# A transformer block on one core: weight loads issued in the written order, dummy matmuls at the start, and a reordered first layer norm

## The chip, the cores and the metric

The kernel runs on one core of one Trainium2 chip. The metric is the device time of one execution in microseconds (us). All engines of the core run their own instruction lists side by side and meet only at semaphores: TensorE (PE in the rows; its weight loads are listed apart as PEld), VectorE (DVE), ScalarE (ACT), GpSimd (POOL), and SyncE (SP), which here only issues DMA transfers. The 16 DMA engines of the core carry out what SP, ACT and POOL issue.

## The reference

One block of a diffusion transformer, for 2 images of 256 tokens of width D = 1152, with 2 heads of 576, in bf16:

```
mod = (silu(c) @ w_mod)            -> shift_a, scale_a, gate_a, shift_m, scale_m, gate_m
h   = layernorm(x) * (1 + scale_a) + shift_a
q, k, v = h @ wqkv                 ; attn = softmax(q k^T / sqrt(576))
x   = x + gate_a * ((attn @ v) @ wo)
h2  = layernorm(x) * (1 + scale_m) + shift_m
out = x + gate_m * (gelu(h2 @ w_fc1) @ w_fc2)
```

w_mod is 1152 x 6912, wqkv 1152 x 3456, wo 1152 x 1152, w_fc1 1152 x 4608, w_fc2 4608 x 1152. Every weight is read once; the whole read is 50 MB.

## The kernel before, in words

**Tiling.** The 512 tokens are four tiles t of 128. The width 1152 is nine pieces kt of 128 rows. A weight slice 1152 x 1152 takes one region of 20736 bytes a partition in the on-chip memory, and regions are used again: region A holds the scale slice of w_mod (`WSC`) and later the query weights (`WQ`); B holds the key weights (`WK`) and later `WO`; C the shift slice (`WSH`) and later the value weights (`WV`); a region of four times that size holds the other four slices of w_mod (`WMODR`) and later `WFC2`; `WFC1` comes back into A and C.

**Stages on TensorE**, in this order: the transposed c (`c_T`); the scale pieces `sc_0` to `sc_8` (each nine matmuls of 2 columns into one bank, one weight piece kt at a time), each followed by one or two dummy matmuls of 512 columns (`warm`), with the transposes of the normalised token tiles (`xnT_0` to `xnT_3`, nine of 128 x 128 each) between them; the first six column tiles of K, kt by kt; K tiles 6 and 7; the shift pieces `sh_0` to `sh_8`; K tile 8; nine tiles of Q (`proj(WQ, ...)`, lines 1006 to 1012) with scores and softmax between them; V; `rows` (line 901), which makes the other four modulation rows out of `WMODR`, kt by kt; attention times V; the output projection `wo`; the second layer norm; fc1 and fc2. K needs only the scale (`hk`, line 798: 18 VectorE pieces), Q and V also the shift (`hx`, lines 842 and 845: 6 pieces on ScalarE, 12 on VectorE).

**The first layer norm** (lines 701 to 737). Tiles 0 to 2 take their statistics on VectorE (three `bn_stats`, one aggregate), tile 3 on ScalarE (a square pass and a sum pass); 1/sqrt comes from GpSimd. Tile 0 is normalised on ScalarE (line 732, with -mean/sigma made in line 730), tiles 1 to 3 on VectorE (line 735).

**What sets the order.** The program is written as a list of units. `Sched.schedule` plays them in time with costs of its own and so fixes each engine's list. TensorE is held to the written order (`pe_seq`). On the other engines the planner takes, among the units whose inputs are ready at that moment of its model, the one with the highest priority. For SP the priority is the written order (`u.bl = 1e12 - u.uid`, line 305), but a load that is not ready yet is passed over. A load is not ready as long as the region that it writes is still read: `WQ` has to wait for the last matmul that reads `WSC`, `WV` for the last one that reads `WSH`, `WO` for K tile 8. `WMODR`'s region is free from the start. In the written order the loads are x, `WSC`, `WK`, `WSH`, `WQ` (two pieces, columns 0 to 383 and 384 to 1151, line 793), `WV` (line 832), `WMODR` (three pieces, line 834), `WO` (line 848), then `WFC1` pieces 0 and 1, 2 and 3, then `WFC2`.

On the chip SP issues its list strictly one after the other, and a DMA that waits for a semaphore holds all that stand behind it. The gate rows (`st_g`, `ld_g`) go out and come back through POOL's own queue.

Of the kernel before, what the change touches and what calls it, by code (L numbers as in the profile page):

```python
# [8 lines left out]
ENGINES = ("pe", "act", "dve", "pool", "sp")  # L9
# [162 lines left out]
class Sched:  # L172
# [107 lines left out]
    def schedule(self, dma_bw=385.0, dma_issue=650.0, dma_lat0=900.0, dma_lat1=600.0, verbose=False):  # L280
        units = self.units
        for u in units:
            for ins in u.instrs:
                for d in ins.deps:
                    if d.unit is not u:
                        u.deps.add(d.unit)
        for u in units:
            for d in u.deps:
                d.succ.add(u)
        pe_seq = [u for u in units if u.eng == "pe"]  # L290
        pe_next = {a.uid: b for a, b in zip(pe_seq, pe_seq[1:])}
        pe_pos = 0
        for u in reversed(units):
            m = 0.0
            for s in u.succ:
                if s.bl > m:
                    m = s.bl
            if u.uid in pe_next:
                m = max(m, pe_next[u.uid].bl)
            d = u.dur if u.dma_bytes == 0 else (u.dur + u.dma_bytes / dma_bw + dma_lat0 + dma_lat1)  # L300
            u.bl = d + m + u.prio_boost
        nsp = sum(1 for u in units if u.eng == "sp")
        for u in units:
            if u.eng == "sp":
                u.bl = 1e12 - u.uid
        ndeps = {u.uid: len(u.deps) for u in units}
        ready = {e: [] for e in ENGINES}
        avail_time = {}
        for u in units:
            if ndeps[u.uid] == 0:  # L310
                avail_time[u.uid] = 0.0
                ready[u.eng].append((-u.bl, u.uid))
        eng_free = {e: 0.0 for e in ENGINES}
        dma_free = 0.0
        events = []
        now = 0.0
        done = 0
        order = {e: [] for e in ENGINES}
        pending_fin = []
        n = len(units)  # L320
        scheduled = 0
        while scheduled < n:
            progressed = False
            for e in ENGINES:
                if eng_free[e] > now:
                    continue
                h = ready[e]
                if not h:
                    continue
                pick = None  # L330
                for it in h:
                    if e == "pe" and it[1] != pe_seq[pe_pos].uid:
                        continue
                    if avail_time[it[1]] <= now and (pick is None or it < pick):
                        pick = it
                if pick is None:
                    continue
                h.remove(pick)
                if e == "pe":
                    pe_pos += 1  # L340
                u = units[pick[1]]
                u.start = now
                if u.dma_bytes > 0:
                    u.end = now + u.dur
                    if e == "sp":
                        xs = max(u.end + dma_lat0, dma_free)
                        dma_free = xs + u.dma_bytes / dma_bw
                        u.fin = dma_free + dma_lat1
                    else:
                        u.fin = u.end + 1500.0 + u.dma_bytes / (dma_bw * 0.5) + dma_lat1  # L350
                else:
                    u.end = now + u.dur
                    u.fin = u.end + u.lat
                eng_free[e] = u.end
                order[e].append(u)
                pending_fin.append((u.fin, u.uid))
                scheduled += 1
                progressed = True
            fin_now = sorted(it for it in pending_fin if it[0] <= now)
            if fin_now:  # L360
                pending_fin = [it for it in pending_fin if it[0] > now]
            for f, uid in fin_now:
                for s in units[uid].succ:
                    ndeps[s.uid] -= 1
                    at = max(avail_time.get(s.uid, 0.0), f + (SEM_LAT if True else 0.0))
                    avail_time[s.uid] = at
                    if ndeps[s.uid] == 0:
                        ready[s.eng].append((-s.bl, s.uid))
                progressed = True
            if progressed:  # L370
                continue
            cands = []
            if pending_fin:
                cands.append(min(it[0] for it in pending_fin))
            for e in ENGINES:
                if eng_free[e] > now:
                    cands.append(eng_free[e])
                for it in ready[e]:
                    if avail_time[it[1]] > now:
                        cands.append(avail_time[it[1]])  # L380
            cands = [c for c in cands if c > now]
            if not cands:
                raise RuntimeError("scheduler stuck: %d/%d" % (scheduled, n))
            now = min(cands)
        self.order = order
        self.makespan = max(u.fin for u in units)
        return order

    def emit(self, nc, block, sems, dma_sems):
        order = self.order  # L390
# [101 lines left out]
D = 1152  # L492
KT = 9
# [27 lines left out]
def c_dve_fast(n):  # L521
    return 160.0 + 0.37 * n
# [10 lines left out]
def build_kernel(nc, x, c, wqkv, wo, w_mod, w_fc1, w_fc2, out):  # L533
# [5 lines left out]
    with (  # L539
# [14 lines left out]
        def ps16(bank, c0=0, n=1024):  # L554
            v = psum[:, bank * 512: (bank + 1) * 512].bitcast(BF16)
            return v[:, c0:c0 + n]
# [94 lines left out]
        def dve(cost, fn, reads, writes, name):  # L651
            return S.op("dve", cost, fn, reads=reads, writes=writes, name=name)
# [37 lines left out]

        S.op("pool", 100, lambda e: e.memset(NHALF, -0.5), writes=[NHALF], name="nhalf")

        CT_PS = ps16(7, 0, 18)
        S.unit("pe", 100, "c_T")
        tr(CT_PS, CSB[0:18, :], IDENT[0:18, 0:18])
# [25 lines left out]
        for t in range(4):  # L721
            xt, xn, mv, rs = X[:, t, :], XN[:, t, :], MV[:, t, :], RSTD[:, t:t + 1]
            if t < 3:
                ln_stats_dve(xt, [X[:, t, i * CH:(i + 1) * CH] for i in range(NCH)], BN[:, t, :], mv, rs, "ln1_%d" % t)
            else:
                ln_stats_act(xt, xn, mv, SUMS[:, 0:2], rs, "ln1_%d" % t)
            m = MV[:, t, 0:1]
            if t == 0:
                nm = NMR[:, t:t + 1]
                dve(170, lambda e, m=m, rs=rs, nm=nm: e.scalar_tensor_tensor(out=nm, in0=m, scalar=-1.0, in1=rs, op0=ALU.mult, op1=ALU.mult),  # L730
                    [m, rs], [nm], "nmr_%d" % t)
                act(1300, lambda e, xt=xt, xn=xn, rs=rs, nm=nm: e.activation(out=xn, in_=xt, func=ACTF.Identity, scale=rs, bias=nm),  # L732
                    [xt, rs, nm], [xn], "xn_%d" % t)
            else:
                dve(c_dve_fast(D), lambda e, xt=xt, xn=xn, m=m, rs=rs: e.tensor_scalar(out=xn, in0=xt, scalar1=m, scalar2=rs,
                                                                                     op0=ALU.subtract, op1=ALU.mult),
                    [xt, m, rs], [xn], "xn_%d" % t)


        XB = [(0, 1, 2), (3, 4, 6)]  # L740
# [10 lines left out]
                src = ps16(XB[b][q], 0, nk * 256).rearrange("p (k t) -> p k t", k=nk)  # L751
                copy_on(eng, HX[:, 4 * q:4 * q + nk, b * 256:(b + 1) * 256], src, nk * 256, True, "xnT_ev%d_%d" % (b, q))

        def warm(n, tag, src):
            for i in range(n):
                S.unit("pe", 300.0, "warm_%s_%d" % (tag, i))
                mm(ps32(5), IDENT, src, True, True)

        def mod_kt(W, kt, col0, name):
            S.unit("pe", 9 * 27.0, name)  # L760
# [1 line left out]
                mm(ps32(7, col0 + f * 2, 2), W[:, kt, f * 128:(f + 1) * 128], ST[:, kt:18:9], kt == 0 and f == 0, kt == KT - 1,  # L762
                   skip_group_check=True)

        mod_kt(WSC, 0, 0, "sc_0")
        warm(1, "a", WSC[:, 0, 0:512])
        xn_T(0)
        mod_kt(WSC, 1, 0, "sc_1")
        warm(1, "b", WSC[:, 1, 0:512])
        mod_kt(WSC, 2, 0, "sc_2")  # L770
        warm(1, "c", WSC[:, 2, 0:512])
        xn_T(1)
        mod_kt(WSC, 3, 0, "sc_3")
        warm(1, "d", WSC[:, 3, 0:512])
        mod_kt(WSC, 4, 0, "sc_4")
        warm(1, "e", WSC[:, 4, 0:512])
        xn_T(2)
        mod_kt(WSC, 5, 0, "sc_5")
        warm(1, "f", WSC[:, 5, 0:512])
        xn_T(3)  # L780
        mod_kt(WSC, 6, 0, "sc_6")
        warm(1, "g", WSC[:, 6, 0:512])
        mod_kt(WSC, 7, 0, "sc_7")
        warm(2, "h", WSC[:, 7, 0:512])
        mod_kt(WSC, 8, 0, "sc_8")
        warm(2, "i", WSC[:, 8, 0:512])
        xn_T_ev(0)
        xn_T_ev(1)
        MT0 = ps32(7, 0, 18)
# [33 lines left out]
            qk_evac(dst_j, bank)  # L823

        dve(330, lambda e: e.memset(QK[64:128, 4, :], 0.0), [], [QK[64:128, 4, :]], "z4a")
        dve(330, lambda e: e.memset(Q4B[0:64, :], 0.0), [], [Q4B[0:64, :]], "z4b")

        proj(WK, 6, 15, HK, 6)
        proj(WK, 7, 16, HK, 0)
# [305 lines left out]
```

## Time and profile before

| what | us |
|---|---|
| median of 3 runs | 276.48 |
| lowest, highest | 275.17, 277.48 |
| the profiled execution's own time | 275.82 |
| its span in the trace | 273.7 |
| TensorE busy in the span | 242.7 |
| VectorE, ScalarE, GpSimd busy | 68.5, 65.6, 19.6 |

All times in the rows are counted from the start of the span; 2.1 us of the execution lie around it. In a timeline a row is: start, duration, engine, line, operation, output <- inputs, count, and in brackets how long the engine was idle before and who released it. A row with a count above one stands for that many neighbouring instructions. In the list of transfers the last number is the time from the issue to the landing. The chain of waits is followed back from the last instruction; "issue" in it is time for which the trace shows no releaser.

### The profile page before, as it was taken

How to read it: one execution, taken by the hardware profiler on the slowest of the kernel's cores; microseconds unless marked ns; L12 is line 12 of the kernel's file. 1: busy time of each engine (PE TensorE's matmuls, PEld its weight loads, DVE VectorE, ACT ScalarE, POOL GpSimd, SP SyncE). 2: the span in 40 equal slices, each digit the busy share in tenths (PEclk: the TensorE clock that was granted, in tenths of full speed). 3: DMA queues.
4: the chain of work that ended last, by engine and by line, in shares of the span. 5: the costliest groups of instructions: out<-in, count | busy, mean ns of one | idle time of the engine just before them, and what ended most of it. 6: DMA issues, size and time to landing. Idle time of an engine off the chain costs nothing.

```text
span 273.7 us, 3973 instructions
## 1 busy us (share of the span) xinstructions
PE 242.7 (89%) x1734; PEld 143.8 (53%) x1746; DVE 68.5 (25%) x183; ACT 65.6 (24%) x128; POOL 19.6 (7%) x33
## 2 busy tenths in 40 slices
PE   0589980079989999999999999999999999999996
PEld 0464450034656557666976444444456666666675
DVE  5534231011534024689310000000001221111222
ACT  2540232002226225036953332323210000000000
POOL 1200000000000013575000000000000000000000
PEclk9999996569999999999999999999999999999999
DMA  6999999999664199993079644500000000000001
GB/s 223 387 392 399 428 415 424 379 378 392 244 203 146 25 398 394 389 364 120 0 264 362 188 121 152 166 0 0 2 0 14 17 14 29 17 14 14 17 16 29
DMA packets 27867, 51.57 MB, mean 188 GB/s; under 512 B 1479, under 2 KB 15559, under 8 KB 26699
## 3 DMA queue, kind: packets, MB, share of 16 engines
q1 hardware_dynamic: 27440, 50.14, 51.1%
q0 software_dynamic: 384, 1.19, 1.2%
q8 instruction: 13, 0.21, 0.3%
q14 instruction: 3, 0.02, 0.0%
q10 hardware_dynamic: 27, 0.00, 0.0%
HBM read 50.14 MB, written 1.19 MB: 188 GB/s over the span
## 4 chain that ended last, share of the span: by engine, by line
PE 88%; issue 6%; DVE 2%; DMA 2%; ACT 1%; SPq 0%
PE psum L667 85%; PE psum L670 3%; DMA arena<-in_x_dram 2%; DVE arena L845 1%; ACT arena L712 0%; ACT arena L732 0%; SPq L648 0%; DVE arena L990 0%; ACT arena L662 0%; DVE arena L971 0%; DVE arena L798 0%; DVE arena L1078 0%; DVE arena L1079 0%; ACT arena L713 0%; DVE arena L790 0%
## 5 line engine op out<-in xcount | busy, mean ns | idle before, releaser
L667 PE MATMUL psum<-arena 128*128 128x384 bf16 (+5 forms) x1627 | 237.0, 311 | 24.7 <-issue 16.1
L667 PEld LDWEIGHTS psum<-arena 128*128 128x128 bf16 (+1 forms) x1639 | 136.5, 98 | 120.9 <-issue 20.0
L1078 DVE TENSOR_TENSOR arena<-psum,arena 128x384 f32<-128x384 f32 (+1 forms) x14 | 7.0, 501 | 118.6 <-PE psum L667 118.6
L662 ACT ACTIVATE arena<-psum 128x512 bf16<-128x512 f32 (+6 forms) x34 | 19.0, 579 | 61.2 <-PE psum L667 61.2
L1003 ACT ACTIVATE arena<-psum 128x512 bf16<-128x512 f32 (+1 forms) x44 | 22.4, 523 | 43.3 <-PE psum L667 43.3
L664 DVE CAST arena<-psum 128x512 bf16<-128x512 f32 (+3 forms) x17 | 10.7, 643 | 48.9 <-PE psum L667 48.8
L670 PE MATMUL psum<-arena 128*128 128x128 bf16 (+2 forms) x107 | 9.6, 240 | 3.7 <-DMA arena<-in_c_dram 2.2
L972 POOL TENSOR_TENSOR arena<-arena 128x384 f32<-128x384 f32 x12 | 10.9, 910 | 10.1 <-DVE arena L971 9.0
L670 PEld LDWEIGHTS psum<-arena 128*128 128x128 bf16 (+2 forms) x107 | 8.0, 112 | 6.2 <-DMA arena<-in_c_dram 2.2
L704 DVE BATCH_NORM_STATS2 arena<-arena 128x6 f32<-128x384 f32 (+1 forms) x21 | 10.8, 543 | 0.4 <-DMA arena<-in_x_dram 0.4
L977 ACT ACTIVATE arena<-arena 128x1152 bf16<-128x1152 f32 x4 | 5.4, 1350 | 9.6 <-DVE arena L976 9.5
L971 DVE TENSOR_TENSOR arena<-psum,arena 128x384 f32<-128x384 f32 x12 | 6.6, 549 | 3.7 <-PE psum L667 3.6
L648 POOL DMA_DIRECT2D dit_scratch<-arena x2 | 1.3, 629 | 86.9 <-DVE arena L664 86.9
L1079 DVE TENSOR_TENSOR arena<-arena 128x384 bf16<-128x384 f32 (+1 forms) x14 | 7.0, 502 | 0.5
L993 ACT ACTIVATE arena<-psum,arena 128x128 bf16<-128x128 bf16 x16 | 6.1, 460 | 4.2 <-PE psum L670 4.0
L990 DVE TENSOR_SCALAR arena<-psum,arena 128x128 bf16<-128x128 bf16 x20 | 5.5, 335 | 4.5 <-PE psum L670 4.5
L870 ACT ACTIVATE arena<-psum,arena 128x256 bf16<-128x256 f32 x8 | 3.7, 470 | 7.7 <-DVE arena L867 4.9
L708 POOL TENSOR_TENSOR arena<-arena 128x1 f32<-128x1 f32 x7 | 3.9, 550 | 8.6 <-DVE arena L707 8.6
L866 DVE TENSOR_REDUCE arena<-psum 128x2 f32<-128x512 f32 x4 | 2.8, 692 | 6.0 <-PE psum L667 5.9
L842 ACT ACTIVATE arena<-arena 128x256 bf16<-128x256 bf16 x6 | 3.1, 586 | 4.3 <-DVE arena L836 4.3
L664 DVE COPY arena<-psum 128x256 bf16<-128x256 bf16 (+2 forms) x5 | 2.0, 423 | 6.6 <-PE psum L667 4.7
L798 DVE TENSOR_SCALAR arena<-arena 128x256 bf16<-128x256 bf16 x18 | 3.6, 281 | 0.0
(39 smaller groups left out, 28.0 us busy)
## 6 DMA issues: line engine op xcount, KB each, us to landing
arena<-in_w_mod_dram SPq DMA_DIRECT2D x3, 3456.0 KB, 26.5
arena<-in_w_fc_dram SPq DMA_DIRECT2D x9, 1152.0 KB, 8.1
arena<-in_w_fc_dram SPq DMA_DIRECT2D x4, 2592.0 KB, 14.9
arena<-in_w_mod_dram SPq DMA_DIRECT2D x9, 288.0 KB, 6.5
arena<-in_wqkv_dram SPq DMA_DIRECT2D x9, 288.0 KB, 7.9
arena<-in_w_mod_dram SPq DMA_DIRECT2D x3, 864.0 KB, 13.1
arena<-in_wqkv_dram SPq DMA_DIRECT2D x1, 2592.0 KB, 17.2
arena<-in_wo_dram SPq DMA_DIRECT2D x1, 2592.0 KB, 20.3
```

Of the source, the lines that this page charges most:

```text
L662: act(c_act(n), lambda e: e.activation(out=dst, in_=src, func=ACTF.Copy), [src], [dst], name)
L664: dve(c_dve_psum16(n) if psum16 else c_dve_psum32(n), lambda e: e.tensor_copy(dst, src), [src], [dst], name)
L667: S.instr(lambda e: e.matmul(o, lhsT=l, rhs=r, start=st, stop=sp, **kw), reads=[l, r], writes=[o])
L670: S.instr(lambda e: e.transpose(o, i_, idn), reads=[i_, idn], writes=[o])
L704: dve(550, lambda e, s=s, o=o: e.bn_stats(out=o, in_=s), [s], [o], "bn_%s_%d" % (tag, ci))
L971: dve(550, lambda e, o=o, ga=ga, x1c=x1c: e.tensor_tensor(out=x1c, in0=o, in1=ga, op=ALU.mult), [o, ga], [x1c], "wo_t1_%d_%d" % (t, ci))
L972: S.op("pool", 930, lambda e, xs=xs, x1c=x1c: e.tensor_tensor(out=x1c, in0=x1c, in1=xs, op=ALU.add), reads=[x1c, xs], writes=[x1c], name=" ...
L990: dve(335, lambda e, o=o, dst=dst, s1=s1, s2=s2: e.tensor_scalar(out=dst, in0=o, scalar1=s1, scalar2=s2, op0=ALU.mult, op1=ALU.add), [o, s ...
L993: act(440, lambda e, o=o, dst=dst, s1=s1, s2=s2: e.activation(out=dst, in_=o, func=ACTF.Identity, scale=s1, bias=s2), [o, s1, s2], [dst], ...
L1003: act(c_act(ntok), lambda e: e.activation(out=dst, in_=o, func=ACTF.Gelu_apprx_tanh), [o], [dst], "gelu_%d_%d" % (f, tok0))
L1078: dve(c_dve_psum32(w), lambda e, o=o, gm=gm, t1=t1: e.tensor_tensor(out=t1, in0=o, in1=gm, op=ALU.mult), [o, gm], [t1], "fc2_t1_%d_%d" % ( ...
L1079: dve(c_dve_32(w), lambda e, t1=t1, x1c=x1c, ost=ost: e.tensor_tensor(out=ost, in0=t1, in1=x1c, op=ALU.add), [t1, x1c], [ost], "fc2_out_%d ...
```

## The change

SP is now held to the written order as TensorE was: a load that is not ready holds the later ones in the planner's list. `Q4B` (512 columns, later half of a query tile) is zeroed first on VectorE; two dummy matmuls of 512 columns (identity times `Q4B`) stand before `c_T` and 22 after it, ahead of the first transposes. The dummy matmuls between the scale pieces read `Q4B` and no longer `WSC`: one after each piece and one at the end, and the transposes of tiles 1, 2, 3 follow `sc_1`, `sc_3`, `sc_5`. Tile 0 is normalised on VectorE like the others. A report function that runs only when asked for is added; it puts no instruction into the program.

```diff
-        pe_seq = [u for u in units if u.eng == "pe"]
-        pe_next = {a.uid: b for a, b in zip(pe_seq, pe_seq[1:])}
-        pe_pos = 0
+        seq = {e: [u for u in units if u.eng == e] for e in ("pe", "sp")}
+        pos = {"pe": 0, "sp": 0}
+        pe_next = {a.uid: b for a, b in zip(seq["pe"], seq["pe"][1:])}
...
-                    if e == "pe" and it[1] != pe_seq[pe_pos].uid:
+                    if e in seq and it[1] != seq[e][pos[e]].uid:
                         continue
...
-                if e == "pe":
-                    pe_pos += 1
+                if e in seq:
+                    pos[e] += 1
...
+        dve(600, lambda e: e.memset(Q4B, 0.0), [], [Q4B], "zq4b")
+        for i in range(2):
+            S.unit("pe", 430.0, "warm_a%d" % i)
+            mm(ps32(5), IDENT, Q4B, True, True)
...
-            if t == 0:
-                nm = NMR[:, t:t + 1]
-                dve(170, lambda e, m=m, rs=rs, nm=nm: e.scalar_tensor_tensor(out=nm, in0=m, scalar=-1.0, in1=rs, op0=ALU.mult, op1=ALU.mult),
-                    [m, rs], [nm], "nmr_%d" % t)
-                act(1300, lambda e, xt=xt, xn=xn, rs=rs, nm=nm: e.activation(out=xn, in_=xt, func=ACTF.Identity, scale=rs, bias=nm),
-                    [xt, rs, nm], [xn], "xn_%d" % t)
-            else:
-                dve(c_dve_fast(D), ...)
+            dve(c_dve_fast(D), lambda e, xt=xt, xn=xn, m=m, rs=rs: e.tensor_scalar(out=xn, in0=xt, scalar1=m, scalar2=rs,
+                                                                                 op0=ALU.subtract, op1=ALU.mult),
+                [xt, m, rs], [xn], "xn_%d" % t)
...
-        def warm(n, tag, src):
+        def warm(n, tag):
             for i in range(n):
-                S.unit("pe", 300.0, "warm_%s_%d" % (tag, i))
-                mm(ps32(5), IDENT, src, True, True)
+                S.unit("pe", 215.0, "warm_%s_%d" % (tag, i))
+                mm(ps32(5), IDENT, Q4B, True, True)
...
-        mod_kt(WSC, 0, 0, "sc_0")
-        warm(1, "a", WSC[:, 0, 0:512])
+        warm(22, "b")
         xn_T(0)
-        mod_kt(WSC, 1, 0, "sc_1")
-        warm(1, "b", WSC[:, 1, 0:512])
...
-        mod_kt(WSC, 8, 0, "sc_8")
-        warm(2, "i", WSC[:, 8, 0:512])
+        for kt in range(KT):
+            mod_kt(WSC, kt, 0, "sc_%d" % kt)
+            warm(1, "k%d" % kt)
+            if kt in (1, 3, 5):
+                xn_T((kt + 1) // 2)
+        warm(1, "e")
...
-        dve(330, lambda e: e.memset(Q4B[0:64, :], 0.0), [], [Q4B[0:64, :]], "z4b")
```

## Rows read from the trace of the kernel before

**Rows 1.** The page: shares of the chain that ended last, by engine.

```profile
PE 88%; issue 6%; DVE 2%; DMA 2%; ACT 1%; SPq 0%
```

**Rows 2.** The chain of waits in order: start, duration, what, count.

```profile
14.62 0.88 PE psum L667 x10
15.50 0.96 PE psum L670 x9
...
19.05 0.70 PE psum L667 x10
...
42.43 13.77 issue
...
121.86 0.50 PE psum L670 x9
...
146.40 10.74 PE psum L667 x49
```

**Rows 3.** Timeline of TensorE's matmuls, 0 to 60 us.

```profile
20.52 19.81 PE L667 MATMUL psum<-arena 128*128 128x512 bf16 x160 [0.43 <-DVE arena L798]
56.20 3.98 PE L667 MATMUL psum<-arena 128*128 128x512 bf16 x10 [15.87 <-issue]
```

**Rows 4.** Timeline of SP's issues: last of WSC and WSH, WMODR, then WQ.

```profile
7.68 0.43 SPq L648 DMA_DIRECT2D arena<-in_w_mod_dram  x1
...
13.90 0.50 SPq L648 DMA_DIRECT2D arena<-in_w_mod_dram  x1
...
21.29 2.11 SPq L648 DMA_DIRECT2D arena<-in_w_mod_dram  x1
...
23.45 3.80 SPq L648 DMA_DIRECT2D arena<-in_wqkv_dram  x1
...
27.29 23.10 SPq L648 DMA_DIRECT2D arena<-in_wqkv_dram  x1
```

**Rows 5.** Transfers of rows 4 to landing; then WV, and a lone WFC2 piece.

```profile
arena<-in_w_mod_dram SPq DMA_DIRECT2D x1, 288.0 KB, 6.6
...
arena<-in_w_mod_dram SPq DMA_DIRECT2D x1, 864.0 KB, 14.4
...
arena<-in_w_mod_dram SPq DMA_DIRECT2D x1, 3456.0 KB, 32.1
...
arena<-in_wqkv_dram SPq DMA_DIRECT2D x1, 864.0 KB, 32.7
...
arena<-in_wqkv_dram SPq DMA_DIRECT2D x1, 1728.0 KB, 33.6
...
arena<-in_wqkv_dram SPq DMA_DIRECT2D x1, 2592.0 KB, 17.2
...
arena<-in_w_fc_dram SPq DMA_DIRECT2D x1, 2592.0 KB, 9.6
```

**Rows 6.** Busy time by stretch; last three columns: granted clock, DMA share, GB/s.

```profile
24.00:30.00 6.00, 5.95 (x28) 2.73 (x28) 0.00 (x0) 0.00 (x0) 0.00 (x0) 1.00 1.06 421
...
42.00:56.00 14.00, 0.00 (x0) 0.00 (x0) 0.42 (x2) 0.79 (x2) 0.00 (x0) 0.52 1.03 397
...
58.00:60.00 2.00, 2.00 (x7) 0.66 (x6) 0.00 (x0) 0.00 (x0) 0.00 (x0) 0.60 1.06 380
```

**Rows 7.** Timeline of the first 12 us: identity, 1/sigma, tiles 0 and 3 normalised.

```profile
1.10 0.29 POOL L687 TENSOR_SCALAR_AFFINE_SELECT arena<-arena 128x128 bf16<-128x128 bf16 x1
...
5.79 0.56 POOL L708 TENSOR_TENSOR arena<-arena 128x1 f32<-128x1 f32 x1 [4.40 <-DVE arena L707]
...
9.35 1.33 ACT L732 ACTIVATE arena<-arena 128x1152 bf16<-128x1152 bf16 x1
...
10.99 0.58 DVE L735 TENSOR_SCALAR arena<-arena 128x1152 bf16<-128x1152 bf16 x1 [0.44 <-POOL arena L719]
```

**Rows 8.** Timeline around 100 us: weight loads of rows, first wo product on VectorE.

```profile
91.79 4.16 PEld L667 LDWEIGHTS psum<-arena 128*2 128x2 bf16 x108 [0.32 <-issue]
...
110.20 0.56 DVE L971 TENSOR_TENSOR arena<-psum,arena 128x384 f32<-128x384 f32 x1 [0.31 <-PE psum L667]
```

More of the change, by code (lines that the diff above doesn't have):

```diff
@@ L387, in schedule, with report @@
         return order
+    def report(self):
+        print("model makespan %.1f" % (self.makespan / 1000))
+        for e in ENGINES:
+            print(e, "%.1f" % (sum(u.end - u.start for u in self.order[e]) / 1000))
     def emit(self, nc, block, sems, dma_sems):
@@ L727, in build_kernel @@
             m = MV[:, t, 0:1]
-            if t == 0:
-                nm = NMR[:, t:t + 1]
-                dve(170, lambda e, m=m, rs=rs, nm=nm: e.scalar_tensor_tensor(out=nm, in0=m, scalar=-1.0, in1=rs, op0=ALU.mult, op1=ALU.mult),
-                    [m, rs], [nm], "nmr_%d" % t)
-                act(1300, lambda e, xt=xt, xn=xn, rs=rs, nm=nm: e.activation(out=xn, in_=xt, func=ACTF.Identity, scale=rs, bias=nm),
-                    [xt, rs, nm], [xn], "xn_%d" % t)
-            else:
-                dve(c_dve_fast(D), lambda e, xt=xt, xn=xn, m=m, rs=rs: e.tensor_scalar(out=xn, in0=xt, scalar1=m, scalar2=rs,
-                                                                                     op0=ALU.subtract, op1=ALU.mult),
-                    [xt, m, rs], [xn], "xn_%d" % t)
+            dve(c_dve_fast(D), lambda e, xt=xt, xn=xn, m=m, rs=rs: e.tensor_scalar(out=xn, in0=xt, scalar1=m, scalar2=rs,
+                                                                                 op0=ALU.subtract, op1=ALU.mult),
+                [xt, m, rs], [xn], "xn_%d" % t)
         XB = [(0, 1, 2), (3, 4, 6)]
@@ L763, in mod_kt @@
                    skip_group_check=True)
-        mod_kt(WSC, 0, 0, "sc_0")
-        warm(1, "a", WSC[:, 0, 0:512])
+        warm(22, "b")
         xn_T(0)
-        mod_kt(WSC, 1, 0, "sc_1")
-        warm(1, "b", WSC[:, 1, 0:512])
[L770 to L784, printed above, removed]
-        mod_kt(WSC, 8, 0, "sc_8")
-        warm(2, "i", WSC[:, 8, 0:512])
+        for kt in range(KT):
[4 more added lines that the diff above has]
+        warm(1, "e")
         xn_T_ev(0)
```

## Prediction

> **What bounds the kernel now.** I read the shares of the chain first [rows 1]: TensorE holds 88% of it, and 6% is time without a releaser. In the chain by order of time that 6% is nearly one piece, 13.77 us from 42.43 [rows 2]. TensorE's timeline shows it from the other side: the K matmuls end at 20.52 + 19.81 = 40.33, and the first Q matmul starts at 56.20 after 15.87 us idle [rows 3]. The trace gives no releaser, so I went to SP's list. The last of the three WMODR loads is issued at 21.29, the two WQ loads at 23.45 and 27.29 [rows 4]; their landings come 32.1, 32.7 and 33.6 us later [rows 5], at 53.4, 56.15 and 60.9. The first WQ piece lands 0.05 us before Q starts: Q waits for its weights, which stand behind 3 x 3456 KB that nobody needs before `rows` at 91.79 [rows 8]. The engines that move data are full meanwhile (DMA share 1.03, 397 GB/s from 42 to 56 [rows 6]): the bytes are not too many, they come in the wrong order.
>
> **The order of loads.** WQ must wait for the last read of WSC. Before, the planner found it not ready and passed WMODR ahead; now it stands behind WSH. The last WSH piece lands at 13.90 + 14.4 = 28.3 [rows 4, 5]. The two WQ pieces landed 2.75 and 4.75 us after what stood before them (56.15 - 53.4, 60.9 - 56.15), so I expect them at 31.05 and 35.8. SP now blocks on WQ until `sc_8` is done, at about 16.4 (below); WSC, WK and WSH are issued by then and keep the transfers busy to 28.3, so this wait costs nothing. Q, put before 40.33, then waits only for `hx`, whose end is where the chain's gap begins, 42.43 [rows 2]. Q's ninth matmul reads the last `hx` piece; at 10.74 / 49 = 0.219 us a matmul [rows 2] it would stand at 40.33 + 8 x 0.219 = 42.08, so 0.35 us are lost to `hx`. Saved: 15.87 - 0.35 = **15.5 us**.
>
> **The clock after the gap.** In the gap the granted clock falls to 0.52, and it is 0.60 from 58 to 60 [rows 6], mostly the lower level, 1.2 GHz. The first 10 Q matmuls take 3.98 us [rows 3]; at 0.219 they would take 2.2. Without a gap this loss goes: **1.7 us**, a little under the difference because the last matmul's drain is in the 3.98.
>
> **The start.** It ends with `sc_8`: 19.05 + 0.70 = 19.75 [rows 2], then scale and first `hk` pieces on VectorE, and K at 20.52, 0.77 later. The matmul rate there is of two kinds: ten instructions (a scale piece and a dummy) take 0.88 at 14.62 and 0.70 at 19.05; nine transposes take 0.96 at 15.50 but 0.50 at 121.86 [rows 2]. Most of the stage ran at 1.2 GHz. The new list: two dummies from 1.4, when the identity is done (1.10 + 0.29 [rows 7]; the zeroing of Q4B on VectorE, one memset in the place of one, I cost at nothing, as it lies beside this). c's transpose after them at about 2.4, then 22 dummies. At 1.2 GHz a 512-column matmul costs about 0.43 (10 in 3.98 [rows 3], less the drain). How long do they stay so? No row shows dummies at the start. The nearest is the restart at 56.20: dense 512-column matmuls, slow for the some 3.5 us in which those ten start. By that row the clock rises near 4.9: 6 dummies to 5.0, 16 x 0.219 = 3.5 more, to 8.5. If it never rises, 22 x 0.43 = 9.5, to 11.9.
>
> Tile 0's 1/sigma is ready at 5.79 + 0.56 = 6.35 [rows 7]; normalised on VectorE (0.58, as tile 3's) about 7.2. Before, ScalarE did it at 9.35 to 10.68, behind tile 3's statistics [rows 7]. The first transposes thus wait for the dummies. VectorE gives away the step of line 730 and gets 0.58 more; tile 3, ready at 11.57 [rows 7], comes at worst near 12.1, and its transposes stand near 14. The last WSC piece lands at 7.68 + 6.6 = 14.28 [rows 4, 5], before `sc_8`. So TensorE's own work sets the end: 4 x 0.50 + 8 x 0.70 + 0.45 (`sc_8` without its dummy) = 8.05 after 8.5, that is 16.5, and K at 17.3. Saved against 20.52: **3.2 us**. Bounds: up to 5.0, where the last WSC landing alone sets it (14.28 + 0.45 + 0.77 = 15.5); down to a loss of 3.5, where no matmul gets fast before K (11.9 + 4 x 0.96 + 8 x 0.88 + 0.45 + 0.77 = 24.0). I take 3.2, by the restart row, whose work is of the dummies' kind.
>
> The row on transposes: while they were mixed in, from 14.62 to 16.46, both kinds of work still ran at the slow rate, and the fast rate is first seen at 19.05, behind the last of them [rows 2]. The Trainium skill ("TensorE: Matmul & The Clock Gate", Part 4: PE-mode transpose) says that transposes do not count as work for the clock gate, and so speaks against spreading them through this stage. By that rule the start would save nothing and the sum would be 17.2; the trace neither refutes it nor parts it from the thin 2-column matmuls. It is a rival below.
>
> **What the strict order adds.** WV waits for the last shift matmul, and WMODR and WO now stand behind it on SP. The shift pieces come just before K tile 8, whose nine matmuls end the stage at 40.33: they end near 40.33 - 9 x 0.219 = 38.4, now 35.2. WQ lands at 35.8 by then, so the transfers run low and start anew. A lone 2592 KB took 9.6 [rows 5]: WV at 44.8, long before V is made. WMODR: 3 x 3.54 MB at 421 GB/s [rows 6] = 25.2, to 70.0. `rows` starts at 91.79 - 20.4 = 71.4, and the third piece is asked for after two thirds of its 4.16 [rows 8], at 74.2: 4.2 us to spare. WO (2.65 MB at 397: 6.7) lands at 76.7; the first `wo` product, 110.20 [rows 8], moves to 89.8. WFC1's first pieces, behind WO, and WFC2, now behind WFC1's third and fourth, are wanted later still. POOL's gate transfers keep their queue but meet WO and WFC1 where they met WFC2; with the transfers full in both cases I cost that at nothing; if the gates come late, up to 2 us (the output projection runs ahead by its six banks).
>
> **Sum.** 15.5 + 1.7 + 3.2 = 20.4. From the profiled execution's 275.82 that gives 255.4. The median of the runs is 276.48, 0.66 above it; I predict **255.5**.
>
> **Rivals.**
> (a) The clock falls in the scale stage. The dummies end at 8.5, but the stage runs at the slow rates: 8.5 + 11.3 + 0.77 = 20.6, and the start saves nothing: 275.82 - 17.2 = 258.6. For it: [rows 2] at 14.62 and 15.50. Against: the stage follows 7 us of dense work, and each scale piece keeps a 512-column matmul. 0.20.
> (b) The dummies stay slow to the end. K starts at 24.0: 275.82 - 17.2 + 3.5 = 262.1. Against it stands the restart row. 0.05.
> (c) `rows` waits for WMODR's last piece. Were WV to take 17.2, as before [rows 5], everything behind it lands 7.6 later and eats the 4.2 to spare: 3.4 us, 258.8. For it: the slack is the smallest of the plan. Against: those 17.2 were spent behind WQ's pieces, which are now landed. 0.12.
> (d) Slower than before: SP's strict order itself. WV's wait holds 13.3 MB back until 35.2, and `rows` stops TensorE until they are there. It costs from the moment the stream falls under 13.3 / (74.2 - 35.2) = 341 GB/s, and passes the whole gain when WMODR ends 20.4 after 74.2, that is under 13.3 / 59.4 = 224 GB/s; at 200 GB/s the last piece lands at 101.7, and the time is 255.4 + 27.5 = 282.9. The loaded stretches move 380 to 421 [rows 6]. 0.03.
> (e) The change does not do what it says: WQ still lands late, because its issue hangs on the last read of WSC and the planner's list. The diff holds SP to the written order by index, and no dummy reads WSC any more; only an end of `sc_8` later than 28 would let the transfers run dry. Then only the start would change, 272.6, or by (b) 279.3. 0.02.
>
> **How the numbers follow.** The forecast has 0.58. Its own edge is 252.8: K set by the WSC landing (1.8 better) and the lower runs, some 1 us under the median. Above, the range takes in (a), and (c) in part: to 260.5. About 1% is what a measurement of this kernel can tell from no change. Faster by more than that: the forecast, (a), (b), (c) and half of (e), 0.96; slower: (d) and a share of (e), 0.03; the same: 0.01.
>
> **What would show it.** The changed trace should have no gap of more than 1 us between K and Q; WQ's first piece landing near 31 and the WMODR pieces after WV; Q's first matmuls at the full granted clock, 2.4 GHz; K starting near 17.3; ten instructions of the scale stage in 0.70 and nine transposes in 0.50. If K starts at 20 or later, the start was mis-sized, by (a) or (b) as the dummies' own pitch tells; if TensorE stands still within `rows`, it is (c). A TensorE gap elsewhere between 60 and 110 would mean that I missed a load that SP's order now holds back.

## The result, and the profile after

The changed kernel takes 254.59 us (254.21 to 254.66), the kernel before 276.98 in the runs beside it: a ratio of 0.9193, with a 95% interval of 0.9137 to 0.9249. 255.5 was forecast. The profiled execution took 254.65, its span is 252.8 against 273.7. The medians lie 22.4 us apart and the two spans 20.9, chiefly because the profiled execution of the kernel before, 275.82, was 1.2 under its median.

The share of "issue" in the chain, 6% before [rows 1], is 1% now. Page, shares by engine:

```profile
PE 95%; DVE 2%; DMA 1%; issue 1%; ACT 0%
```

The chain of waits in order (start, duration, what, count) has no hole between K and Q. Against [rows 2] the piece to compare is the one at 42.43, which is gone; what stands near it is VectorE's `hx` (now line 832):

```profile
3.11 6.71 PE psum L672 x22
9.82 0.50 PE psum L675 x9
10.33 0.67 PE psum L672 x19
...
35.49 2.66 DVE arena L832 x10
38.15 0.05 issue
38.20 7.81 PE psum L672 x35
46.01 0.05 issue
46.06 8.61 PE psum L672 x49
```

TensorE's timeline, read to 42 us (start, duration, operation, count). K, the shift pieces and the first Q matmuls are one run of 183 matmuls from 16.76 without a gap, in the place of the two rows of [rows 3]:

```profile
3.05 6.78 PE L672 MATMUL psum<-arena 128*128 128x512 bf16 x22
...
16.76 25.58 PE L672 MATMUL psum<-arena 128*128 128x512 bf16 x183 [0.43 <-DVE arena L786]
```

SP's issues of WQ (two), WV and the third WMODR piece, which answer to [rows 4]:

```profile
15.79 3.30 SPq L653 DMA_DIRECT2D arena<-in_wqkv_dram  x1
...
19.13 6.22 SPq L653 DMA_DIRECT2D arena<-in_wqkv_dram  x1
...
35.27 0.37 SPq L653 DMA_DIRECT2D arena<-in_wqkv_dram  x1
...
36.89 2.73 SPq L653 DMA_DIRECT2D arena<-in_w_mod_dram  x1
```

and the same transfers from issue to landing (last number), for [rows 5]:

```profile
arena<-in_wqkv_dram SPq DMA_DIRECT2D x1, 864.0 KB, 15.4
...
arena<-in_wqkv_dram SPq DMA_DIRECT2D x1, 1728.0 KB, 16.6
...
arena<-in_wqkv_dram SPq DMA_DIRECT2D x1, 2592.0 KB, 10.7
...
arena<-in_w_mod_dram SPq DMA_DIRECT2D x1, 3456.0 KB, 34.1
```

Add each issue to its landing time: WQ is there at 31.2 and 35.7, WV at 46.0, the third WMODR piece at 71.0. Before, WQ landed at 56.15 and 60.9, WMODR at 53.4. The bytes are the same; WQ and WMODR have changed places.

In the stretches (last three columns: granted clock, DMA share, GB/s) the transfers do run low before WV is issued at 35.27, and TensorE's clock stays at 1.00, 2.4 GHz, where [rows 6] had 0.52:

```profile
30.00:36.00 6.00, 5.92 (x100) 3.87 (x100) 1.89 (x5) 1.31 (x4) 0.00 (x0) 1.00 0.68 241
36.00:42.00 6.00, 5.89 (x27) 2.37 (x26) 3.35 (x12) 3.62 (x8) 0.00 (x0) 1.00 0.94 326
```

**Where the 20.9 us came from.** Take one marker of the chain: the piece of 8.61 us and 49 matmuls, which begins within Q's fifth tile, is at 66.92 before and at 46.06 now, 20.86 earlier. 3.76 of it is there when K starts (20.52 to 16.76); the other 17.10 lie between K's start and the marker. Behind it nothing more is won or lost.

### The profile page after: what moved, and what is told of

It reads as the page before. It is cut to its first block, busy times and chain, and to the rows that moved or that the text cites. A ratio compares the mean times of both kernels' runs of the same rounds, so it can differ in the third digit from the quotient of the medians.

```text
span 252.8 us, 4016 instructions
## 1 busy us (share of the span) xinstructions
PE 245.5 (97%) x1756; PEld 143.8 (57%) x1769; DVE 68.9 (27%) x183; ACT 64.3 (25%) x127; POOL 19.6 (8%) x33
## 4 chain that ended last, share of the span: by engine, by line
PE 95%; DVE 2%; DMA 1%; issue 1%; ACT 0%
PE psum L672 93%; PE psum L675 2%; DVE arena L832 1%; DMA arena<-in_c_dram 1%; DVE arena L977 0%; ACT arena L667 0%; DVE arena L958 0%; DVE arena L786 0%; DVE arena L1065 0%; DVE arena L1066 0%; DVE arena L813 0%; DVE arena L778 0%; DVE arena L823 0%
## 5 line engine op out<-in xcount | busy, mean ns | idle before, releaser
L672 PE MATMUL psum<-arena 128*128 128x384 bf16 (+5 forms) x1649 | 241.2, 312 | 4.1 <-POOL arena L692 1.4
L672 PEld LDWEIGHTS psum<-arena 128*128 128x128 bf16 (+1 forms) x1662 | 138.0, 97 | 103.0 <-issue 3.1
L990 ACT ACTIVATE arena<-psum 128x512 bf16<-128x512 f32 (+1 forms) x44 | 22.4, 523 | 43.4 <-PE psum L672 43.3
L675 PEld LDWEIGHTS psum<-arena 128*128 128x128 bf16 (+2 forms) x107 | 6.4, 97 | 3.3 <-DMA arena<-in_c_dram 1.4
L675 PE MATMUL psum<-arena 128*128 128x128 bf16 (+2 forms) x107 | 7.6, 209 | 0.6 <-DMA arena<-in_c_dram 0.5
L786 DVE TENSOR_SCALAR arena<-arena 128x256 bf16<-128x256 bf16 x18 | 3.6, 280 | 0.0
L832 DVE TENSOR_SCALAR arena<-arena 128x256 bf16<-128x256 bf16 x12 | 3.2, 341 | 0.0
## 6 DMA issues: line engine op xcount, KB each, us to landing
arena<-in_w_fc_dram SPq DMA_DIRECT2D x4, 2592.0 KB, 20.5
```

Of the source, the lines that this page charges most:

```text
L672: S.instr(lambda e: e.matmul(o, lhsT=l, rhs=r, start=st, stop=sp, **kw), reads=[l, r], writes=[o])
L675: S.instr(lambda e: e.transpose(o, i_, idn), reads=[i_, idn], writes=[o])
L832: dve(260, lambda e, tgt=tgt, s1=s1, s2=s2: e.tensor_scalar(out=tgt, in0=tgt, scalar1=s1, scalar2=s2, op0=ALU.mult, op1=ALU.add), [tgt, s1 ...
L990: act(c_act(ntok), lambda e: e.activation(out=dst, in_=o, func=ACTF.Gelu_apprx_tanh), [o], [dst], "gelu_%d_%d" % (f, tok0))
```

## The experiments

Each is the changed kernel with one edit, but the first, which is the kernel before with one, and the sixth, which has two. Times are medians; each ratio is to the kernel before, timed beside it. Experiments 1 to 4, 5 to 8, and 9 and 10 ran on three chips, and none of them has the changed kernel timed beside it. The changed kernel's own ratio is known to 0.0056 either way, 1.5 us; differences of about a microsecond from it are not clear of noise by the times alone.

A yardstick for the start: up to K, TensorE has the same list in the changed kernel and in experiments 2, 9 and 10. K starts at 16.76, 17.35, 15.98 and 16.36 in their traces. Rows of experiments 9 and 10:

```profile
15.98 40.07 PE L672 MATMUL psum<-arena 128*128 128x512 bf16 x258 [0.43 <-DVE arena L786]
...
16.36 40.07 PE L672 MATMUL psum<-arena 128*128 128x512 bf16 x258 [0.43 <-DVE arena L786]
```

In each, K starts 7.10 after the first transposes (9.66, 10.25, 8.88, 9.26). What differs is when the dummies end: c's transpose between them came at 2.4 to 2.9, and they turned fast at 6.9, 8.1, 5.9 and 6.7 us, after 11, 14, 10 and 12 slow ones. So two single traces whose K starts lie less than 1.4 us apart show nothing by that alone.

**1. The order of the loads alone.** The planner's three edits of the diff, in the kernel before; only SP's list changes.

> The kernel before with SP alone held to the written order; the lists of all other engines are those of before. Theory (the order of the loads is worth 17.2 us: the gap before Q and the slow Q matmuls behind it): K still starts at 20.5, Q follows at once near 40.4, the time is 17.0 to 17.5 us under before, near 259.4. Rival (the gap goes only together with the early start, because SP's wait for the end of the scale pieces lets the transfers run dry): a gap of several us stays before Q, and the time is 263 or more.

Measured: 258.34 us, 0.9323 (0.9295 to 0.9350). TensorE's timeline, first transposes and K with all that follows without a gap:

```profile
11.20 1.14 PE L670 MATMUL psum<-arena 128*128 128x128 bf16 x9 [2.19 <-ACT arena L732]
...
19.61 40.07 PE L667 MATMUL psum<-arena 128*128 128x512 bf16 x259 [0.43 <-DVE arena L798]
```

From K to the marker it is 48.92 - 19.61 = 29.31, as in the changed kernel (46.06 - 16.76 = 29.30), where before had 46.40. So the order is worth 17.1 by itself, as the theory said; the wait of SP costs Q nothing. The median is 18.6 under the one beside it, more than the 17.5 that the theory allowed; K's start, which moved too, can be part of it. K came 0.9 earlier than expected because the matmuls turned fast nearer to 15.8 than to 18.8; the trace's last store was waited for 1 us longer, so its span, 256.7, shows 17.0 in all.

**2. The start alone.** The changed kernel with the old planner; every list but SP's is that of the changed kernel.

> The changed kernel with the old planner for SP; every other engine's list is that of the changed kernel, and the three WMODR loads are again ahead of WQ. Theory (the start's 3.8 us are worth nothing while Q waits for a landing that the transfers alone set): K starts near 16.8, but Q's first matmul stays near 56, the gap grows to about 19.6 us, and the time is that of before within 1 us. Rival (the two parts add up, each with its own share): Q starts near 52.4, and the time is 3.8 us under before, near 273.

Measured: 276.06 us, 0.9968 (0.9950 to 0.9986). TensorE's timeline:

```profile
17.35 19.81 PE L672 MATMUL psum<-arena 128*128 128x512 bf16 x159 [0.43 <-DVE arena L786]
56.64 3.60 PE L672 MATMUL psum<-arena 128*128 128x512 bf16 x10 [19.48 <-issue]
```

K is 3.2 earlier than before, and the gap is 3.6 longer: the theory. The two parts don't add up as shares: 18.6 us for the order alone, 0.9 for the start alone, 22.4 for both. The start has a worth only where Q no longer waits for a landing.

**3. No dummies ahead of the transposes.** `warm_a` and `warm(22, "b")` taken out.

> The changed kernel without the 24 dummy matmuls ahead of the first transposes; those between the scale pieces stay. Theory (the dummies pay because the stage then runs at the upper clock): the transposes start near 7.6 instead of 9.8, but the stage runs at the slow rates (nine transposes in 0.96) for most of its length, K starts at 18.5 to 19.7, and the time is 1.7 to 3 us above the changed kernel, 256.3 to 257.6. Rival (the dummies only hold the transposes up, and the gain of the start comes from tile 0's normalisation on VectorE): K starts at 16.8 or earlier, and the time is 254.6 or less.

Measured: 255.06 us (254.44 to 255.76), 0.9206 (0.9177 to 0.9235). TensorE's timeline:

```profile
7.54 1.14 PE L675 MATMUL psum<-arena 128*128 128x128 bf16 x9 [4.43 <-DVE arena L713]
...
14.66 0.72 PE L675 MATMUL psum<-arena 128*128 128x128 bf16 x9
...
17.38 40.07 PE L672 MATMUL psum<-arena 128*128 128x512 bf16 x259 [0.43 <-DVE arena L782]
```

Neither theory: the stage is slow, 1.14 for nine transposes until the fourth group at 14.66, but it begins 2.1 earlier (7.54 against 9.66), and K is only 0.6 later than in the changed kernel's trace, within the 1.4 of the yardstick; the medians, 0.5 apart, don't tell them apart either. No worth of the 24 dummies is shown.

**4. No dummies between the scale pieces.** `warm(1, "k%d" % kt)` taken out.

> The changed kernel without the dummy behind each scale piece (the 24 ahead and the one at the end stay). Theory (once risen, the clock stays up through these 6 us whatever runs): the stage loses nine matmuls of 0.216, as far as the landing of the last scale weights at 14.1 allows, K starts at 15.1 to 15.6, all K matmuls are fast, and the time is 1.2 to 1.7 us under the changed kernel, near 253.2. Rival (transposes and 2-column matmuls do not keep the clock up, the rule of the Trainium skill's page TensorE: Matmul & The Clock Gate, Part 4, weighed in the prediction): the rates fall to 0.96 for nine transposes within the stage, or the first K matmuls run at 0.43 each for some 3.5 us, K starts at 16.5 or later, and the time is 1 to 3 us above the changed kernel.

Measured: 253.66 us (252.97 to 255.52), 0.9165 (0.9131 to 0.9198). TensorE's timeline:

```profile
10.33 0.67 PE L675 MATMUL psum<-arena 128*128 128x128 bf16 x9
...
13.27 0.66 PE L675 MATMUL psum<-arena 128*128 128x128 bf16 x9
...
15.64 40.06 PE L672 MATMUL psum<-arena 128*128 128x512 bf16 x259 [1.02 <-DVE arena L785]
```

The theory: the last group of transposes is as fast as the first, and the K matmuls take 40.06 as in the other kernels. In some 4 us of nothing but transposes and 2-column matmuls the rate did not fall. The median is 0.9 under the changed kernel, less than the theory's 1.2 and not clear of noise; against experiment 3, timed beside it, it is 1.4 under, with times that overlap.

**5. Fewer dummies ahead.** `warm(22, "b")` becomes `warm(13, "b")`.

> The changed kernel with 13 dummies after c's transpose in the place of 22; nothing else differs but TensorE's list. Theory (the dummies last until 9.8 while tile 0 is ready at 7.6, so nine of them only hold the stage up, and 15 are enough for the clock, which rose near 6.9): the transposes start near 7.9 to 8.3 at the fast rate, the last scale weights (14.1) set the end, K starts at 15.1 to 15.5, and the time is 1.2 to 1.7 us under the changed kernel, near 253.2. Rival (the clock needs the whole run of dummies): the transposes take 0.96 for nine, K starts at 16.8 or later, and the time is 254.6 or more.

Measured: 253.40 us (253.19 to 253.95), 0.9155 (0.9132 to 0.9179). TensorE's timeline:

```profile
2.64 4.47 PE L672 MATMUL psum<-arena 128*128 128x512 bf16 x13
7.57 0.68 PE L675 MATMUL psum<-arena 128*128 128x128 bf16 x9 [0.45 <-DVE arena L716]
...
11.21 0.68 PE L675 MATMUL psum<-arena 128*128 128x128 bf16 x9 [0.50 <-DVE arena L737]
...
15.30 40.07 PE L672 MATMUL psum<-arena 128*128 128x512 bf16 x263 [0.43 <-DVE arena L786]
```

The theory in its times, with K at 15.30, under all four starts of the yardstick. The transposes now wait 0.45 for tile 0 and not for dummies. What the theory took for the limit, the landing of the last scale weights, is not on the chain: it runs through the third group of transposes, which waits 0.50 for VectorE to normalise tile 2.

**6. The same, with the shift pieces ahead of K tile 7.**

```diff
+        for kt in range(KT):
+            mod_kt(WSH, kt, 18, "sh_%d" % kt)
         proj(WK, 7, 16, HK, 0)
-        for kt in range(KT):
-            mod_kt(WSH, kt, 18, "sh_%d" % kt)
```

> The 13 dummies, and the shift pieces moved ahead of K tile 7, so that two K tiles stand beside VectorE's and ScalarE's 18 hx pieces. In the changed kernel the first Q matmuls are held up by hx (seven weight loads waited 1.6 us in all). Theory: TensorE no longer waits for hx, Q's first tile is 0.4 to 0.8 us faster, the V load is issued 2 us earlier, and the time is 0.4 to 0.8 us under the kernel with 13 dummies alone, near 252.6. Rival (the shift weights, which landed at 28.6, are late for shift pieces at 28.9): TensorE waits there, and nothing is gained.

Measured: 252.79 us (252.69 to 252.92), 0.9130 (0.9105 to 0.9155). TensorE's timeline, and the 40.07 of the same run of matmuls is 39.48:

```profile
15.39 39.48 PE L672 MATMUL psum<-arena 128*128 128x512 bf16 x263 [0.40 <-DVE arena L786]
```

The waits of TensorE's weight loads for `hx` (line 832, 1.6 us in all in the changed kernel) no longer appear. The theory: 0.6 us under experiment 5, timed beside it, and the two sets of times do not overlap. This version has the lowest time of all.

**7. Tile 0 on ScalarE again.** The branch `if t == 0` of the kernel before put back.

> The changed kernel with tile 0 normalised on ScalarE again, as before the change. Theory (the earlier tile 0 is what moved the start, the dummies only fill the time): tile 0 is ready near 11.2, the first transposes start 1.4 us later than in the changed kernel, K starts near 18.2, and the time is 1.0 to 1.6 us above the changed kernel, near 256. Rival (the dummies carry the start; tile 0's engine does not matter): K starts within 0.5 us of 16.8, and the time is 254.6 within 0.5.

Measured: 255.87 us (255.21 to 257.77), 0.9253 (0.9220 to 0.9286). TensorE's timeline:

```profile
10.39 0.68 PE L675 MATMUL psum<-arena 128*128 128x128 bf16 x9 [0.66 <-ACT arena L741]
...
17.29 40.07 PE L672 MATMUL psum<-arena 128*128 128x512 bf16 x263 [0.43 <-DVE arena L793]
```

In the profiled run, 255.21, K is 0.5 later, nearer to the rival; the median is 1.3 above the changed kernel's, as the theory had it, but with a wide spread and not clear of noise. The theory's way is seen (the transposes wait for ScalarE, 0.66 behind the dummies), but tile 0 came at 10.4 and not at 11.2: ScalarE begins it at 9.00, behind both passes of tile 3's statistics, as in the kernel before, where it began at 9.35 [rows 7].

**8. No dummy at all.**

> The changed kernel without any dummy matmul, ahead or between. Theory (only 512-column work lifts the clock in time; transposes and 2-column matmuls do not): the stage runs at the slow rates from 7.6 to about 15.5, K starts near 16.4, and its first matmuls run at 0.43 each for 3 to 5 us, so that the K stage takes 1.5 to 2.5 us longer; the time is 1 to 2.5 us above the changed kernel, 255.6 to 257. Rival (the thin work lifts the clock as well, as it stood at the fast rate from 14.7 in the run without dummies ahead): K starts at 15.1 to 16.4 with fast matmuls, and the time is 253.2 to 254.3, under the changed kernel.

Measured: 255.01 us (254.59 to 255.76), 0.9218 (0.9191 to 0.9245). TensorE's timeline:

```profile
7.73 1.14 PE L675 MATMUL psum<-arena 128*128 128x128 bf16 x9 [4.94 <-DVE arena L734]
...
12.58 1.12 PE L675 MATMUL psum<-arena 128*128 128x128 bf16 x9
...
15.48 41.38 PE L672 MATMUL psum<-arena 128*128 128x512 bf16 x263 [0.85 <-DVE arena L780]
```

By mechanism the theory: all four groups of transposes are slow, and the same K matmuls take 41.38 in the place of 40.07, 1.3 us more. But K starts 1.3 earlier than in the changed kernel's trace, so that the traces come out even; the medians are 0.4 apart, which is not clear of noise and under what the theory gave. Here the landing of the last scale weights is on the chain (14.2). Experiment 5, timed beside it, is 1.6 faster, and the two sets of times do not overlap: 15 dummies ahead, which end before tile 0 is ready, and those between are worth that much.

**9. WO written ahead of WMODR.** The line of the WO load stands before the loop that loads WMODR.

> The changed kernel with WO written ahead of the three WMODR loads, 2592 KB more in front of them. In the changed kernel the third WMODR piece landed at 71.0 and rows asks for it near 73.7, so the slack measured there is 2.7 us (forecast: 4.2). Theory (the price of a late WMODR is what passes the slack, one for one): the piece lands 6.7 later, at 77.7, TensorE stands still for about 4.0 us within rows, and the time is 4 us above the changed kernel, near 258.6. Rival (rows hangs on the landing of all three from its start, or the slow clock after the halt adds to it): 6 us or more above. Other rival (there is more slack than the rows say): under 2 us above.

Measured: 259.90 us (258.98 to 260.31), 0.9391 (0.9366 to 0.9416). TensorE's timeline (from the halt in `rows` to the transposes behind it) and, below it, the stretch around the end of the halt:

```profile
77.35 7.76 PE L672 MATMUL psum<-arena 128*2 128x384 bf16 x63 [4.09 <-DMA arena<-in_w_mod_dram]
85.04 0.52 PE L675 MATMUL psum<-arena 2*128 2x2 bf16 x18
```

```profile
76.00:80.00 4.00, 2.65 (x36) 1.16 (x36) 0.00 (x0) 0.00 (x0) 0.00 (x0) 0.69 1.10 350
```

The changed kernel has the same transposes here:

```profile
79.92 0.52 PE L675 MATMUL psum<-arena 2*128 2x2 bf16 x18
```

Between the theory and its first rival: TensorE waits 4.09 within `rows`, as reckoned, and behind the halt the granted clock is low (0.69 from 76 to 80). From K's start to these transposes it is 85.04 - 15.98 = 69.06 against 79.92 - 16.76 = 63.16, a price of 5.9, of which 1.8 come from the slow stretch. The medians show 5.3, which fits K's start, 0.8 earlier here. So the slack of WMODR in the changed kernel was real and small, under 3 us.

**10. WMODR written ahead of WV**, behind WQ.

> The changed kernel with the WMODR loads written ahead of WV, as the planner had them, but behind WQ; SP keeps the written order. The transfers then do not run dry before the shift pieces end. Theory (what counts is which matmuls a load is ahead of, not that the transfers are always full): WQ lands as before and Q has no gap, but WV lands near 36 + 25 + 7 = 68 instead of 46, while the first V matmul stands at 57.5: TensorE waits 10 us there and 1 to 2 us more for the slow clock behind it, and the time is 11 to 12 us above the changed kernel, near 266. Rival (a full queue makes up for it: everything behind WV comes earlier, so the wait is won back later): under 5 us above.

Measured: 267.63 us (265.99 to 267.87), 0.9654 (0.9626 to 0.9682). TensorE's timeline:

```profile
67.76 8.52 PE L672 MATMUL psum<-arena 128*128 128x384 bf16 x47 [11.33 <-DMA arena<-in_wqkv_dram]
```

The theory, a little dearer: 11.3 us of waiting for WV, and 8.52 for the 47 matmuls that took 6.74 in the changed kernel's chain. The transfers were full from 20 us to WV's landing at 67.7 (DMA share 1.03), and it gained nothing: what was loaded early was not what TensorE came to first.

## Why the prediction was right

**The order of loads, and the clock after the gap: right.** 15.5 + 1.7 = 17.2 were forecast; both traces give 17.1 from K to the marker, and experiment 1 gives 17.1 with that edit alone. WQ was to land at 31.05 and 35.8 and landed at 31.2 and 35.7. The granted clock at Q is 1.00.

**The start: right in sum, by two terms that were off in opposite ways; that they cancelled is luck.** 3.2 was forecast, 3.76 measured in this pair of traces. The old list of the start has K at 20.52 and, in experiment 1, at 19.61, the new one at 15.98 to 17.35: other pairs would have given 2.3 to 4.5. The dummies were to end at 8.5; they ended at 9.82, because c's transpose came at 2.9 and because the matmuls turned fast near 6.9, not 4.9 (the weight loads in the trace stand 0.43 apart until then). The restart row was the right kind of row and the wrong length: eight of its matmuls were slow, here eleven dummies were. The stage was to take 8.05 and took 6.16 (9.82 to 15.98): two scale pieces and a dummy take 0.67 at the upper clock, where I had 0.70 for one piece and a dummy. The row at 19.05 that I took for the rate runs to the drain of its last matmul, which VectorE waits for: it is not the time from one group to the next.

**What made the start earlier** was not parted in the prediction. Experiments 1, 3 and 7 part it, as far as single traces can: with neither dummies ahead nor tile 0 on VectorE, K starts at 19.6 to 20.5; with VectorE alone at 17.4, with dummies alone at 17.3, with both at 16.0 to 17.4. Each alone does most of it, in its own way. In the kernel before, the first transposes of tokens stand at 10.73:

```profile
10.73 1.14 PE L670 MATMUL psum<-arena 128*128 128x128 bf16 x9 [1.52 <-ACT arena L732]
```

With VectorE alone they start 3.2 earlier (7.54), and from them to K it is as long as before, 9.8. With dummies alone they start about as before (10.39), and it is 6.9 to K. The two do not add up, since tile 0 is ready at 7.6 and the dummies stand in its way until 9.8. With 13 of them K starts at 15.30 and 15.39 (experiments 5 and 6). The new place of the transposes among the scale pieces is in the changed kernel and in experiments 3 and 7 alike and was not taken out alone; its share is open. I had noted that the first transposes wait for the dummies and did not ask what fewer would give.

**The rivals.** (a), the clock falling within the stage, did not come: nine transposes take 0.50 in the chain at 9.82. Experiment 4 takes the dummies between the scale pieces out and it still holds. Experiment 8 shows the other half: with thin matmuls and transposes alone, from 7.7 to 14.6, the rate did not rise. The Trainium skill ("TensorE: Matmul & The Clock Gate", Part 4: PE-mode transpose) says that transposes don't count as work for the gate. For the rise experiment 8 agrees, so far as transposes and 2-column matmuls can be told together; that they, and the 2-column matmuls with them, would lose a clock already risen was my own reading, in the rival of experiment 4 too, and experiment 4 is against it for its 4 us. (b) did not come. (c), `rows` waiting for WMODR, did not come: the piece landed at 71.0 (forecast 70.0), `rows` began near 70.9 (71.4), so the slack was about 2.7 and not 4.2; experiment 9 spent it and more, and paid. (d), the strict order as a loss, has a true mechanism, as experiment 10 shows for another order: 13 us above the changed kernel, and still under before. (e) did not come: WQ's first piece landed at 31.2.

The gates over POOL's queue were costed at nothing, and nothing is seen of them: the marker and the chain's last long piece, 70.77 us at 200.36 before and at 179.50 after, are both 20.86 apart.

## What to carry to other kernels

A gap without a releaser, in which the transfers are full, was here a question of order: list what lands before the missing load and ask when each is first read. A planner that passes over a load because it is not ready yet may put megabytes ahead of it; a strict order removes that, and is then only as good as the order written, so reckon the slack of every load behind a waiting one. Two repairs of the same wait did not add up here: time each alone, then ask for the smallest that does. And before a small difference between two traces is explained, see how far traces of one and the same list lie apart.

## What the runs showed of the hardware that was not expected

The column of the granted clock reads 1.00 from the start of every trace, also while 512-column matmuls stand 0.43 apart and nine transposes take 1.14; for the first stretch only the durations tell the level. With one and the same list, the start's dense 512-column matmuls turned fast at 5.9 to 8.1 us in four traces, and K's start is spread over 1.4 us. In experiment 4 the matmuls stayed fast through about 4 us of transposes and 2-column matmuls. That the changed kernel's 34 dummies are worth anything together is not shown (experiment 8); with 13 in the place of 22 they are worth 1.6 us (experiments 5 and 8). SP's issue of one transfer was itself held for 23.10 us behind 10.6 MB [rows 4]; in the changed kernel the same issue took 6.22.
